# Layer 1's output product: the sums of two gate quarters made by accumulating DRAM transfers instead of VectorE

## The chip, the cores and the metric

The kernel runs on one core of a Trainium2 chip. The metric is the device time of one execution in microseconds (us), as a median over runs. The engines are TensorE (PE; its weight loads are PEld), VectorE (DVE), ScalarE (ACT), GpSimd (POOL) and SyncE (SP), which here issues nearly all transfers; a "q" behind an engine's name is its instruction queue.

## The reference

Causal attention with a decay, followed by two feed-forward layers. All is float32.

```python
def reference(**kwargs):
    attn_out = _attn_ref(**attn_kwargs)          # 4 batches, 8 heads, 576 positions, 64 wide
    B, H, S, D = attn_out.shape
    x = np.ascontiguousarray(attn_out.transpose(0, 2, 1, 3)).reshape(B * S, H * D)   # 2304 x 512
    x = _moe_ref(x=x, **moe_kwargs)              # h = x @ w_in; max(0.01 h, h) @ w_out, 512 -> 2048 -> 512
    return _moe2_ref(x=x, **moe2_kwargs)         # h = x @ w_in; (h * sigmoid(h)) @ w_out
```

## The kernel before

Tokens are processed in five stages that overlap: attention per head; the hidden product of layer 1 with its gate (line 960); the output product of layer 1 (line 1218); and the two products of layer 2 (lines 1525 and 1667). Each float32 operand of a product is split into a rounded part (a copy on ScalarE) and a residual (a subtraction on VectorE), and a product is three passes: rounded by rounded, and twice rounded by residual.

The hidden product runs over eight chunks of 256 or 320 tokens and 16 blocks of 128 features. It starts while attention is still running and fills TensorE's time between the heads. After each pair of blocks `gate` stores 128 x 2 x n gate values to the DRAM tensor `g1_d` (line 1055), 64 stores in all; `g1_d` has eight slabs (a slab is a pair of feature blocks), each over 2304 tokens.

The output product uses a scheme of seven products in place of eight. The tokens are cut into three groups of 768 (n = 0, 1, 2). A group's gate values are cut into quarters: "11" and "21" are the first and second 384 tokens with the first half of the features (slabs 0 to 3), "12" and "22" the same tokens with the second half (slabs 4 to 7). Each quarter comes as four pieces (s = 0 to 3) of 128 x 2 x 384 values, 384 KB, which `quarters` loads from `g1_d` (line 1091, tile gq). From them `made` and `prep` build the seven left operands, in place:

- operand 1 is "11", operand 2 is "12", operand 4 is "22";
- operand 5 is "21" + "22" (line 1117, the first operation of `made`);
- operand 6 is operand 5 minus "11" (line 1120);
- operand 7 is "22" minus operand 6 (line 1140), operand 3 is "12" minus operand 6 (line 1164).

All of these run on VectorE through the helper `sub`, so that the profile shows them under line 1357 (gq from gq): 16 per group, 48 in all. `prep` then splits each piece into the tile gs (line 1151 on ScalarE; the residual through the helper `less`, line 373, on VectorE). Four split buffers go round; a buffer comes free when TensorE has used it.

There are three sets of quarter buffers (`q_group`). "11" always uses set 0. "21" and "12" of a group use one and the same set, and "22" the other; the two change places from group to group. So "21" of group n+1 is loaded into the buffers that "22" of group n leaves, and "22" of group n+1 into those that "12" of group n leaves. "12" is used last in a group, by operand 3. The order of the loads is "11", "21", "22" of a group, with "12" of the group before it in front.

The order of all instructions on every engine is fixed when the program is built. A planner (`Plan`) plays the whole kernel through with a cost for every operation; coroutines (`hidden`, `quarters`, `preps`, `summed` and others) wait for signals, take buffers, and hand operations with a rank to an engine; the planner writes them out in the order in which the engines come free in its own time. A subtraction that may run on either VectorE or GpSimd goes to the one that would end it first. On the chip, each queue runs strictly in that order, and an instruction that waits holds up all behind it on its queue. The order of the seven operands of a group is in `G_TURN`: for the groups 1 and 2 it is 1, 6, 5, 2, 7, 4, 3.

GpSimd makes some key residuals for attention (line 369) until the end of attention, and nothing after that. It issues no transfer.

Of the kernel before, what the change touches and what calls it, by code (L numbers as in the profile page):

```python
# [13 lines left out]
ALU = mybir.AluOpType  # L14
# [43 lines left out]
)  # L58
SPLITS = 4
INPUT_AT = 5  # L60
X_ON = "d"
SET_B = ("h", "h", ("acc", 0), ("acc", 1))


# [8 lines left out]
TB = 384  # L73
# [14 lines left out]
class Plan:  # L88
# [90 lines left out]
    def wait(self, *names):  # L179
        def step(resume):  # L180
            missing = [n for n in names if n not in self.seen]
            if not missing:
                resume()
                return
            left = [len(missing)]

            def one():
                left[0] -= 1
                if not left[0]:
                    resume()  # L190

            for n in missing:
                self.waiting.setdefault(n, []).append(one)

        return step
# [8 lines left out]
    def signal(self, name):  # L204
        self.seen[name] = True
        for fn in self.waiting.pop(name, []):
            fn()
# [79 lines left out]
def fused_kernel(ctx, tc, qt, kt, va, vb, ft, w1, wi2, wo2, out):  # L287
    nc = tc.nc
# [8 lines left out]
    SF = FF // 4  # L297
# [769 lines left out]
    def quarter(grp, s):  # L1067
        return w2t["q", Q_AT[grp] + s // 2][:, s % 2]

    def q_group(n, name):  # L1070
        return {"11": 0, "21": 1 + n % 2, "12": 1 + n % 2, "22": 2 - n % 2}[name]

    def quarters():

        yield wait("decoded")
        todo = [(0, "11"), (0, "21"), (0, "22")]
        for n in range(NG):
            todo += [(n, "12")]
            if n + 1 < NG:
                todo += [(n + 1, "11"), (n + 1, "21"), (n + 1, "22")]  # L1080
        for n, name in todo:
            i, j = int(name[0]) - 1, int(name[1]) - 1
            o = (2 * n + i) * TB
            grp = q_group(n, name)
            for s in range(SF):
                sg = j * SF + s
                yield wait(*[("g1", k, sg) for k, (o1, n1) in enumerate(CHUNKS) if o1 < o + TB and o1 + n1 > o])
                yield take(("q", grp, s), 1)

                def load(n, name, s, sg, o, t):  # L1090
                    yield dma(393e3, lambda: nc.sync.dma_start(out=t, in_=g1_d[sg, :, :, o:o + TB]), 0)
                    signal(("q", n, name, s))

                p.start(load(n, name, s, sg, o, quarter(grp, s)))

    g_order = sorted((7 * n + pos, n, q) for n in range(NG) for q, pos in G_TURN[n])
    gx = {}
# [14 lines left out]

    def made(n, s):

        a11, a21, a22 = (quarter(q_group(n, k), s) for k in ("11", "21", "22"))
        yield wait(("q", n, "21", s), ("q", n, "22", s))
        yield sub(2 * TB, a21, a21, a22, X_ON, 0, ALU.add)
        signal(("x5", n, s))
        yield wait(("gx", n, 1, s))
        yield sub(2 * TB, a11, a21, a11, "d", 0)  # L1120
        signal(("x6", n, s))
        q_used(n, "21", s, 2)

    def prep(n, q, s, i):
        a = {k: quarter(q_group(n, k), s) for k in ("11", "12", "21", "22")}
        t = w2t["s", i % SPLITS]
        src, name = None, None
        if q == 1:
            yield wait(("q", n, "11", s))
            src = a["11"]  # L1130
        elif q == 5:
            yield wait(("x5", n, s))
            src = a["21"]
        elif q == 6:
            yield wait(("x6", n, s))
            src = a["11"]
        elif q == 7:
            yield wait(("x6", n, s))
            yield wait(("x3", n, s))
            yield sub(2 * TB, a["11"], a["22"], a["11"], "d", 0)  # L1140
            src = a["11"]
        elif q == 4:
            yield wait(("q", n, "22", s))
            src = a["22"]
        elif q == 2:
            yield wait(("q", n, "12", s))
            src = a["12"]
        else:
            yield wait(("x3", n, s))
            src = a["12"]  # L1150
        yield act(2 * TB, lambda: nc.scalar.copy(t[:, 0], src), 0, 0.09)  # L1151
        yield less(2 * TB, t[:, 1], src, f32(t[:, 0]), "d", 0, PE_LAT)
        gx[n, q, s] = t, i
        signal(("gx", n, q, s))
        if q == 5:
            q_used(n, "21", s, 2)
        elif q == 7:
            q_used(n, "22", s, 2)
            q_used(n, "11", s, 1)
        elif q == 4:  # L1160
            q_used(n, "22", s, 2)
        elif q == 2:
            yield wait(("x6", n, s))
            yield sub(2 * TB, a["12"], a["12"], a["11"], "d", 0)
            yield wait(("gx", n, 6, s))
            signal(("x3", n, s))
        elif q == 3:
            q_used(n, "12", s, 1)
# [802 lines left out]
        decp["wo"] = wo_es.enter_context(tc.tile_pool(name="wop", bufs=1))  # L1971

    with tc.manual_schedule():
        for gen in (opening(), first_weights(), loads(), attention(), hidden(), quarters(), preps(), summed(), all_fills(),
                    second_input(), second_weights(), hidden2(), second_values(), summed2()):
            p.start(gen)
        p.run()
# [51 lines left out]
```

## Time and profile before

| | |
|---|---|
| median of 3 runs | 960.33 us (959.15 to 962.2) |
| profiled execution, whole | 963.02 us |
| its span, first to last instruction | 961.3 us |
| TensorE busy | 940.9 us (98%) |
| VectorE busy | 753.1 us (78%) |
| ScalarE busy | 610.8 us (64%) |
| GpSimd busy | 56.5 us (6%) |
| moved by transfers | 196.8 MB |

Times are from the start of the span. Durations are from the one profiled execution. A matmul's end is modelled, so that a busy TensorE may still have matmuls that run slowly. The granted clock is given as a share of full speed. The DMA share is the mean busy share of the 16 transfer engines; it can come out slightly above 1.

The output product of layer 1 lies between 392 and 607 us. Until 419 us hidden-product work is mixed into it, and from 578 us on the first product of layer 2.

### The profile page before, as it was taken

To read this page: it belongs to the slowest core of one execution; us is meant where nothing else is said; L and a number is where in the kernel's file an instruction comes from. 1 tells how busy PE (TensorE), PEld (TensorE's weight loads), DVE (VectorE), ACT (ScalarE), POOL (GpSimd) and SP (SyncE) were. 2 spreads that over 40 slices of the span, in tenths; PEclk is the share of its full clock that TensorE was granted. 3 is DMA by queue.
4 is the path that set the end of the run, shared out by engine and by line. 5 is a ranking of instruction groups with operands and counts; after the bars stand their busy time and mean duration, and the time that the engine had idled before them with its cause. 6 is when DMAs were issued, how large, how long until landed. Compare 5 with 4: busy or idle time off the path is not lost.

```text
span 961.3 us, 18261 instructions
## 1 busy us (share of the span) xinstructions
PE 940.9 (98%) x6483; PEld 891.6 (93%) x6483; DVE 753.1 (78%) x1782; ACT 610.8 (64%) x1382; POOL 56.5 (6%) x71
## 2 busy tenths in 40 slices
PE   9999999999999999999989999999999999999998
PEld 7777998999888889999989899999999999999998
DVE  6998786689688962979999779858544498888885
ACT  7978787788588854666546359547556674444442
POOL 2001221122022100000000000000000000000000
PEclk9999999999999999999999999999999999999999
DMA  7943553466777656994956685797766683544542
GB/s 202 290 136 89 165 168 95 131 227 215 243 223 241 194 166 224 370 359 161 344 206 185 221 256 177 266 325 236 287 218 208 221 261 112 152 132 139 147 127 72
DMA packets 160023, 196.80 MB, mean 205 GB/s; under 512 B 9638, under 2 KB 145982, under 8 KB 159900
## 3 DMA queue, kind: packets, MB, share of 16 engines
q1 hardware_dynamic: 159500, 195.24, 63.5%
q8 instruction: 51, 0.84, 0.3%
q10 hardware_dynamic: 432, 0.39, 0.1%
q14 instruction: 40, 0.33, 0.1%
HBM read 125.94 MB, written 69.65 MB: 203 GB/s over the span
## 4 chain that ended last, share of the span: by engine, by line
PE 68%; DVE 13%; DMA 9%; ACT 5%; issue 3%; SPq 2%; POOL 0%; DVEq 0%; ACTq 0%; POOLq 0%
PE m L1667 18%; PE m L1525 18%; PE acc L1218 10%; PE hpw L960 10%; PE sps L743 4%; PE av L892 4%; PE tps L824 3%; DMA gq<-g_d 3%; DVE gq L1357 2%; DMA wst<-in_wi_dram 2%; ACT sc L766 1%; DVE sc L723 1%; DVE gs L373 1%; ACT sc L776 1%; PE hps L960 1%
## 5 line engine op out<-in xcount | busy, mean ns | idle before, releaser
L960 PE MATMUL hpw<-ring,w 128*128 128x320 f32 (+1 forms) x1344 | 218.0, 303 | 0.1
L960 PEld LDWEIGHTS hpw<-ring,w 128*128 128x128 f32 x1344 | 191.0, 190 | 2.4 <-issue 1.4
L1218 PE MATMUL acc<-gs,w 128*128 128x384 f32 x1008 | 186.2, 344 | 7.1 <-DVE gs L373 5.4
L1218 PEld LDWEIGHTS acc<-gs,w 128*128 128x128 f32 x1008 | 180.5, 191 | 10.2 <-DVE gs L373 6.5
L1525 PE MATMUL m<-xc,w 128*128 128x384 f32 x1008 | 180.3, 339 | 0.6 <-ACT m L1551 0.6
L1525 PEld LDWEIGHTS m<-xc,w 128*128 128x128 f32 x1008 | 177.6, 188 | 1.4 <-ACT m L1551 1.0
L1667 PE MATMUL m<-w,gc 128*128 128x256 f32 x1512 | 178.6, 280 | 0.0
L1667 PEld LDWEIGHTS m<-w,gc 128*128 128x128 f32 x1512 | 178.4, 188 | 0.0
L358 ACT CAST gc<-g 128x512 fp32r<-128x512 f32 (+1 forms) x180 | 80.0, 490 | 86.7 <-DVE g L1357 52.2
L1151 ACT CAST gs<-gq 128x768 fp32r<-128x768 f32 x84 | 69.8, 836 | 61.0 <-PE acc L1218 31.2
L766 ACT ACTIVATE sc<-sc,st 128x576 f32<-128x576 f32 (+4 forms) x160 | 92.9, 581 | 24.6 <-DVE st L723 23.6
L723 DVE CUSTOM_DVE_ANT_0 sc<-sps,zmask 128x288 f32<-128x288 f32 (+4 forms) x160 | 71.0, 448 | 31.1 <-PE sps L743 23.8
L373 DVE TENSOR_TENSOR gs<-gq,gs 128x768 fp32r<-128x768 f32 x84 | 79.4, 952 | 17.5 <-ACT gs L1151 16.9
L373 DVE TENSOR_TENSOR gc<-g,gc 128x512 fp32r<-128x512 f32 (+1 forms) x180 | 89.8, 525 | 3.3 <-ACT gc L358 1.9
L824 PE MATMUL tps<-ident,sc 66*107 66x66 f32 (+3 forms) x480 | 68.0, 269 | 3.8 <-ACT sc L776 1.8
L1357 DVE TENSOR_TENSOR g<-g 128x256 f32<-128x256 f32 x144 | 58.3, 418 | 16.7 <-DMA g<-g_d 16.2
L743 PE MATMUL sps<-m,s 66*128 66x288 f32 (+9 forms) x288 | 67.4, 315 | 3.2 <-DMA g_d<-gw 1.7
L369 POOL TENSOR_TENSOR m<-qk,m 64x288 fp32r<-64x288 f32 (+1 forms) x56 | 51.4, 930 | 275.2 <-ACT m L358 145.0
L373 DVE TENSOR_TENSOR w<-w 128x512 fp32r<-128x512 f32 x84 | 55.6, 686 | 14.6 <-ACT w L1915 14.4
L824 PEld LDWEIGHTS tps<-ident,sc 66*107 66x107 f32 (+3 forms) x480 | 55.2, 151 | 10.9 <-ACT sc L776 3.6
L1915 ACT CAST w<-w 128x512 fp32r<-128x512 f32 x84 | 50.7, 620 | 19.0 <-DMA w<-w_d 18.3
L1053 ACT ACTIVATE gw<-hpw 128x320 f32<-128x320 f32 (+1 forms) x112 | 44.7, 409 | 27.0 <-PE hpw L960 23.5
(124 smaller groups left out, 1113.3 us busy)
## 6 DMA issues: line engine op xcount, KB each, us to landing
w<-w_d SPq DMA_DIRECT2D x84, 256.0 KB
gq<-g_d SPq DMA_DIRECT2D x48, 384.0 KB
g_d<-z SPq DMA_DIRECT2D x24, 768.0 KB
g<-g_d SPq DMA_DIRECT2D x36, 512.0 KB
w_d<-f SPq DMA_DIRECT2D x16, 896.0 KB
g_d<-gw SPq DMA_DIRECT2D x32, 320.0 KB
wst<-in_w_dram SPq DMA_DIRECT2D x17, 512.0 KB
g_d<-gw SPq DMA_DIRECT2D x32, 256.0 KB
```

Source lines behind the costliest of these rows:

```text
L358: ("act", act_cost(n, base), lambda: nc.scalar.copy(dst, src), 0.0),
L373: ("dve", dve_cost(n), lambda: nc.vector.tensor_tensor(dst, a, b, op=ALU.subtract), 0.0),
L723: yield dve(w, lambda: nc.vector.tensor_tensor_reduce(out=sc[0:qn, k0:k0 + w], in0=ps[0:qn], in1=zmask[0:qn, z0:z0 + w], scale=-0.125, sca ...
L743: nc.tensor.matmul(ps[0:qn], ht[x][:, qs], ht[y][:, k0:k0 + w], start=r == 0, stop=r == len(ops) - 1)
L766: yield act(kn, lambda: nc.scalar.activation(sc[0:qn, 0:kn], sc[0:qn, 0:kn], ACTF.Exp, scale=-1.0, bias=st[0:qn, 2 * i + a:2 * i + a + 1], ...
L824: nc.tensor.transpose(ps[0:k1 - k0, o:o + qn], ht["p"][i][0:qn, k0:k1], ident[0:qn, 0:qn])
L960: nc.tensor.matmul(dst, w[:, wi, c * 128:(c + 1) * 128], x(xi, c), start=(first_ and c == 0 and r == 0), stop=(c == KC - 1 and r == 2), sk ...
L1151: yield act(2 * TB, lambda: nc.scalar.copy(t[:, 0], src), 0, 0.09)
L1218: nc.tensor.matmul(dst, w[:, e, wi, j * 128:(j + 1) * 128], x[:, xi, e], start=start and s == 0 and e == 0 and r == 0, stop=stop and s == ...
L1357: ("dve", dve_cost(n), lambda: nc.vector.tensor_tensor(dst, a, b, op=op_), 0.0),
L1525: nc.tensor.matmul(dst, w[:, wi, c * 128:(c + 1) * 128], x[:, xi, c], start=start and c == 0 and r == 0, stop=stop and c == 1 and r == 2, ...
L1667: nc.tensor.matmul(banks[b][:, e], t[:, gi, a * 128:(a + 1) * 128], w[:, wi], start=begin and a == 0 and r == 0, stop=jp == NP // 2 - 1 an ...
```

## The change

The sum "21" + "22" is no longer made on VectorE. A new coroutine `added` issues, for each group and piece, one transfer from GpSimd's queue that adds the piece of "22" in `g1_d` to the piece of "21" in `g1_d`, in DRAM: twelve transfers of 384 KB. Each waits for the gate stores of both pieces. The planner counts 1.1 us of GpSimd and 10 us to the landing. `added` is started ahead of `quarters`.

The load of "21" now waits for its sum in place of the gate stores and brings operand 5 directly. In `made` the first VectorE operation goes, and with it the wait for the load of "22"; operand 6 needs "21" and the split of operand 1. Operand 5 needs only the load of "21".

```diff
+    def g1_made(n, i, sg):
+        o = (2 * n + i) * TB
+        return [("g1", k, sg) for k, (o1, n1) in enumerate(CHUNKS) if o1 < o + TB and o1 + n1 > o]
+
+    def added():
+        for n in range(NG):
+            o = (2 * n + 1) * TB
+            for s in range(SF):
+                yield wait(*g1_made(n, 1, s), *g1_made(n, 1, SF + s))
+                yield op("pool", 1.1, lambda: nc.gpsimd.dma_start(
+                    out=g1_d[s, :, :, o:o + TB], in_=g1_d[SF + s, :, :, o:o + TB], accum_op=ALU.add), 0, 10.0)
+                signal(("sum21", n, s))
...
-                yield wait(*[("g1", k, sg) for k, (o1, n1) in enumerate(CHUNKS) if o1 < o + TB and o1 + n1 > o])
+                yield wait(*([("sum21", n, s)] if name == "21" else g1_made(n, i, sg)))
...
-        a11, a21, a22 = (quarter(q_group(n, k), s) for k in ("11", "21", "22"))
-        yield wait(("q", n, "21", s), ("q", n, "22", s))
-        yield sub(2 * TB, a21, a21, a22, X_ON, 0, ALU.add)
-        signal(("x5", n, s))
-        yield wait(("gx", n, 1, s))
+        a11, a21 = (quarter(q_group(n, k), s) for k in ("11", "21"))
+        yield wait(("q", n, "21", s), ("gx", n, 1, s))
         yield sub(2 * TB, a11, a21, a11, "d", 0)
         signal(("x6", n, s))
...
         elif q == 5:
-            yield wait(("x5", n, s))
+            yield wait(("q", n, "21", s))
             src = a["21"]
...
-        for gen in (opening(), first_weights(), loads(), attention(), hidden(), quarters(), preps(), summed(), all_fills(),
+        for gen in (opening(), first_weights(), loads(), attention(), hidden(), added(), quarters(), preps(), summed(), all_fills(),
```

## Rows read from the trace of the kernel before

**Rows 1.** The page's first part: busy us, share of the span, instructions.

```profile
PE 940.9 (98%) x6483; PEld 891.6 (93%) x6483; DVE 753.1 (78%) x1782; ACT 610.8 (64%) x1382; POOL 56.5 (6%) x71
```

**Rows 2.** TensorE's timeline: start, us, operation, count, idle before and releaser.

```profile
394.10 0.97 PE L1218 MATMUL acc<-gs,w 128*128 128x384 f32 x4 [0.86 <-DVE w L373]
...
405.38 13.80 PE L960 MATMUL hpw<-ring,w 128*128 128x320 f32 x93
...
445.76 34.33 PE L1218 MATMUL acc<-gs,w 128*128 128x384 f32 x192 [0.97 <-DVE gs L373]
481.06 4.41 PE L1218 MATMUL acc<-gs,w 128*128 128x384 f32 x23 [0.97 <-DVE gs L373]
486.33 0.44 PE L1218 MATMUL acc<-gs,w 128*128 128x384 f32 x1 [0.85 <-ACT gs L1151]
488.07 59.15 PE L1218 MATMUL acc<-gs,w 128*128 128x384 f32 x324 [1.30 <-DVE gs L373]
549.36 29.16 PE L1218 MATMUL acc<-gs,w 128*128 128x384 f32 x155 [2.14 <-DVE gs L373]
```

**Rows 3.** Busy us by stretch; the last three columns: granted clock, DMA share, GB/s.

```profile
150.00:200.00 50.00, 49.90 (x412) 44.06 (x411) 33.66 (x125) 37.16 (x114) 6.12 (x8) 1.00 0.45 138
340.00:350.00 10.00, 9.97 (x78) 8.51 (x77) 3.60 (x8) 1.80 (x6) 0.00 (x0) 1.00 0.92 285
406.00:422.00 16.00, 16.00 (x107) 16.00 (x107) 10.27 (x20) 8.25 (x18) 0.00 (x0) 1.00 1.00 345
430.00:450.00 20.00, 19.03 (x108) 18.70 (x107) 19.83 (x27) 13.46 (x24) 0.00 (x0) 1.00 0.52 186
470.00:488.00 18.00, 14.94 (x81) 13.73 (x79) 17.93 (x27) 8.06 (x12) 0.00 (x0) 1.00 0.69 262
488.00:494.00 6.00, 5.93 (x25) 5.93 (x26) 4.45 (x9) 1.82 (x5) 0.00 (x0) 0.72 0.66 148
547.00:555.00 8.00, 5.86 (x24) 5.65 (x24) 6.74 (x9) 3.23 (x4) 0.00 (x0) 0.79 0.32 97
```

**Rows 4.** VectorE's timeline around the sums: start, us, operation, count, idle before.

```profile
386.27 7.17 DVE L1357 TENSOR_TENSOR gq<-gq 128x768 f32<-128x768 f32 x8 [4.66 <-DMA gq<-g_d]
...
475.98 3.56 DVE L1357 TENSOR_TENSOR gq<-gq 128x768 f32<-128x768 f32 x4
...
480.06 0.95 DVE L373 TENSOR_TENSOR gs<-gq,gs 128x768 fp32r<-128x768 f32 x1
...
543.95 3.56 DVE L1357 TENSOR_TENSOR gq<-gq 128x768 f32<-128x768 f32 x4
```

**Rows 5.** The chain of work that ended last, in order of time: start, us, what.

```profile
343.27 6.40 DMA w_d<-wf
...
409.75 6.62 DMA wst<-in_wi_dram
...
470.95 4.65 DMA gq<-g_d
...
531.82 8.29 DMA gq<-g_d
```

**Rows 6.** Groups by line: count, busy us, mean ns, idle before and its releasers.

```profile
L1357 DVE TENSOR_TENSOR gq<-gq 128x768 f32<-128x768 f32 x48 | 44.1, 950 | 5.7 <-DMA gq<-g_d 5.6
L369 POOL TENSOR_TENSOR m<-qk,m 64x288 fp32r<-64x288 f32 (+1 forms) x56 | 51.4, 930 | 275.2 <-ACT m L358 145.0 <-DMA qk<-in_qt_dram 67.7 <-PE hpw L960 20.0
```

**Rows 7.** Timeline: gate stores (L1055), last "22" load (L1091), GpSimd's last residual.

```profile
195.96 2.89 SPq L1055 DMA_DIRECT2D g_d<-gw  x2
...
329.53 2.15 SPq L1055 DMA_DIRECT2D g_d<-gw  x2
...
343.88 0.62 SPq L1055 DMA_DIRECT2D g_d<-gw  x1
...
421.47 0.52 SPq L1055 DMA_DIRECT2D g_d<-gw  x1
...
539.23 0.52 SPq L1091 DMA_DIRECT2D gq<-g_d  x1
333.41 1.56 POOL L369 TENSOR_TENSOR m<-qk,m 64x288 fp32r<-64x288 f32 x2 [7.58 <-PE hpw L960]
```

More of the change, by code (lines that the diff above doesn't have):

```diff
@@ L60 @@
 INPUT_AT = 5
-X_ON = "d"
 SET_B = ("h", "h", ("acc", 0), ("acc", 1))
```

## The prediction

> **What bounds the kernel now.** I read the page's first part, then the busy time by stretches, then TensorE's timeline in the stage that the change touches, and last what VectorE and the transfers did at its gaps. TensorE is busy 940.9 of 961.3 us [rows 1], so no change outside TensorE can give more than the 20.4 us of its idle time, and what a slow clock costs after idle time. The question is therefore which of its gaps the twelve sums cause. In the first product of the layer-1 output stage (line 1218) the timeline shows six gaps [rows 2]: 0.86 us at 393, 0.97 at 445, then 0.97, 0.85 and 1.30 between 480 and 488, and 2.14 at 547. That is 7.1 us. Five of the six end with a VectorE instruction, the sixth with a ScalarE split. After the last two groups of gaps the granted clock is 0.72 over 488 to 494 and 0.79 over 547 to 555 [rows 3], that is, TensorE ran part of the time at 1.2 instead of 2.4 GHz after it had stood idle. Lost there: 6 x 0.28 = 1.7 us and 8 x 0.21 = 1.7 us. So the stage holds 7.1 + 3.4 = 10.5 us that a better supply could give back.
>
> The gaps of 480 and 547 have the sums right ahead of them. VectorE runs four 128x768 operations on gq in a row from 475.98, and the residual (gs) that ends the TensorE gap at 481.06 starts on VectorE at 480.06, behind them; from 543.95 four more run, right before the gap that ends at 549.36 [rows 2, 4]. Those four at 475.98 are the adds of the second group, and they run so late because they wait for the "22" quarter: in the chain of waits a gq load of 4.65 us ends just before 475.98, and one of 8.29 us just before the operations of 540.14 [rows 5]. The "22" quarter of a group goes into the buffers that "12" of the group before has left, the last to be freed.
>
> **What the change removes.** Of 48 operations on gq, 0.950 us each [rows 6], the twelve adds go: 12 x 0.95 = 11.4 us of VectorE. They are worth only what they hold up.
> - First group: the eight operations from 386.27 to 393.4 [rows 4] are four adds and four subtractions. TensorE still has the hidden product to do until 419, and only the 0.86 us gap at 393 follows. I take the gap: -0.9 us (0 to -0.9). The 0.97 us at 445 I leave in place: the operations ahead of it there are subtractions for operands 7 and 3, which stay.
> - Second group: operands 5 and 6 now need only "21", which lies in the buffers of the older "22" and is loaded before "22" of its own group. So the wait for the late load goes with the adds. The three gaps, 3.1 us, and the clock loss behind them, 1.7: -4.8 us. Between its ends (0 if the next operand is as late, -4.8) I take the whole, because the four adds take 3.56 us of VectorE [rows 4] in just the 18 us (470 to 488) in which VectorE is busy 17.93 [rows 3], more than the 3.1 us of gaps.
> - Third group, by the same reasoning: 2.1 + 1.7 = -3.8 us (0 to -3.8).
> Together -9.5 us. What is late next is the subtraction 21-11, one operation instead of two, behind a load that stands four places further ahead on SP's queue.
>
> **What it adds.** Twelve transfers issued from GpSimd, 384 KB each, that add one piece of DRAM to another. The trace of before has no such transfer, so I bound it. The least is one plain transfer: where the queues are full (406 to 422, share 1.00) they move 345 GB/s [rows 3], so 393,216 bytes take 1.14 us of all 16 engines. The most is three passes (read the addend, read the target, write the target), 3.42 us. I take two passes, 2.3 us, half-way, since a plain load also reads once and writes once.
> - First group: the stores that its sums wait for are the last four of the third chunk, which ends at 195.96 [rows 7], in 50 us with a share of 0.45 [rows 3]: four sums, 9 us, fit in. Cost 0 (with the cover gone, one late transfer; the nearest row is the 6.40 us of the next point).
> - Second group: the sums follow the stores from 329.53 to 343.88 [rows 7], and meet the 896 KB store of folded weights that the chain waits for from 343.27 for 6.40 us [rows 5], in a stretch where the DMA share is 0.92 and VectorE is busy 3.60 of 10 us [rows 3], that is, stands and waits. Three sums start before it lands: from 0 to 3 x 3.42 = 10.3 us. TensorE's order is fixed, so a late softmax shows as a gap. I take one sum, 2.3 us, because the first has some ten emptier microseconds ahead of the store and the last comes behind it.
> - Third group: the stores end at 421.47 [rows 7], in the full stretch. Four sums are 4 x 2.3 = 9.1 us of transfer beside the loads of the second layer's weights, one of which (6.62 us from 409.75) stands in the chain [rows 5]. Covered: VectorE is idle 16 - 10.3 = 5.7 us in 406 to 422, and the share falls to 0.52 from 430 on [rows 3]. The uncovered rest is 3.4 us; from 0 to 4 x 3.42 - 5.7 = 8.0 us; I take half the rest, 1.7, as the last of the four can only start behind 421 and reaches into the emptier stretch.
>
> A sentence of the Trainium skill speaks against the change here: by "DMA: Bandwidth & Descriptors", section "Issuing engines are not separate DMA queues", transfers issued from GpSimd run on the same 16 engines as those of the SP queue and interleave with them. No run here shows that yet, because before has no transfer from GpSimd; by it the costs above stand, and without it they would be nothing and the time 950.8. By "Collectives: The Full Stack", section "The bandwidth ceiling", an add made by the transfer engines needs two source reads and goes at half the rate of a copy; worked out from that and from the row's 1.14 us a sum would be an estimated 2.3 us, and no run shows it yet.
>
> Waits: on GpSimd a sum stands in order before later key residuals (56 of 0.93 us, the engine idle 275 us before them [rows 6]); the last of these starts at 333.41 [rows 7], so only the sums of the first group and one of the second have any behind them, and keys are prepared up to three heads ahead: cost 0, at worst one late transfer, 6.4 us. On SP the load of "21" waits for its sum, and all later loads stand behind it; the last sum of the second group follows a store of 343.88 and the load of "22" right behind "21" is at 470.95; for the third group these are 421.47 and 539.23 [rows 5, 7]. Over 110 us each are enough for any price above. Cost 0.
>
> **Sum.** -9.5 + 2.3 + 1.7 = -5.5 us. The profiled execution took 963.0 us (span 961.3 and 1.7 around it), 2.7 above the median of 960.3; against it the sum gives 957.5, and on the median 954.8: I say 955.
>
> **Rivals.**
> 1. *Slower: the sums starve the stores and loads.* Place: the attention's end at 343 and the full queues of 409 to 430 [rows 3]. If a sum takes p us of all engines and nothing but VectorE's 5.7 us covers it, the cost is 3p + 4p - 5.7. It beats the gain of 9.5 by more than the measuring limit of 2.9 us (0.3%, about what a measurement of this kernel tells from no change) from p = 2.6 us on. At p = 3.0 the cost is 15.3 and the time 960.3 + 5.8 = 966. For it: the full share in 406 to 422, and the one weight buffer of the attention, which makes everything wait for the store. Against: the share of 0.52 behind, and that transfers in two queues need not stand behind each other.
> 2. *No change: the gap gets another owner.* VectorE is busy 19.83 of 20 us in 430 to 450 [rows 3] without a single add, and each group still has twelve subtractions and 28 residuals; if half the gaps come back with other releasers, the gain is 4.7, the cost 4.0, and the time 960. For it: the residuals also wait for ScalarE's splits, as at 486.33 [rows 2]. Against: in 470 to 488 the adds are the difference.
> 3. *The sums cost nothing,* since they fall into spare share: 960.3 - 9.5 = 950.8. For it: 0.45 and 0.52 around. Against: 0.92 and 1.00 where two of the three groups lie.
>
> **Chances.** Forecast (950.9 to 957.4) 0.50; rival 3 0.08; rival 2 0.17; rival 1 0.25. Faster by over 0.3%: 0.50 + 0.08 = 0.58; within: 0.17; slower: 0.25. The range runs from 950, rival 3, to 966, rival 1 at p = 3.0; its own part, for the likeliest case alone, is 951 to 957.4.
>
> **What would show it.** Right: 36 operations on gq instead of 48; no gap of TensorE before operands 5 and 6 of the second and third group, and a clock of 1.00 behind both places; a first product that ends some 7 us earlier counted from its start; a DMA share above 0.92 around 340 and a later end of the 896 KB store there. Wrong: the sums visible for much more than 3.4 us each, gaps around 343 to 360 or 422 to 450 longer than now, key residuals on GpSimd that begin late, or a "21" load that waits for its sum on SP. A slower clock around 350 or 445 would add to rival 1.

## The result and the profile after

The kernel after takes 967.63 us (967.24 to 968.34, 4 runs) against 961.27 us (959.15 to 963.14) of the kernel before: a ratio of 1.007 [1.0048, 1.0091], 0.7% slower. A second series gave 968.72 against 960.73 us (e5_after, below). The prediction said 955, 5.5 us less than before; it is 6.4 us more. Its first rival, 966 us, came within 2 us, in part by luck: it was worked out at 3.0 us for a sum, and it left out a loss that is there. One execution of e3 (below), the profiled one, took 4245 us in place of some 952, and no trace of e3 is read here. In the code of the kernel after the lines stand elsewhere: L1227 for L1218, L372 for L373, L1160 for L1151, L1366 for L1357, L357 for L358, L823 for L824, L891 for L892, L1534 for L1525.

The page's first part and its row for GpSimd's queue (packets, MB, share of 16 engines' time); beside them the group of operations on gq. They answer [rows 1, 6]:

```profile
PE 941.0 (97%) x6483; PEld 890.5 (92%) x6483; DVE 745.4 (77%) x1771; ACT 612.2 (63%) x1382; POOL 65.2 (7%) x82
...
q0 software_dynamic: 3264, 4.72, 3.3%
```

```profile
L1366 DVE TENSOR_TENSOR gq<-gq 128x768 f32<-128x768 f32 x36 | 33.9, 953 | 0.9 <-DMA gq<-g_d 0.6
```

VectorE does what was planned: 36 operations for 48, and their idle time in front falls from 5.7 to 0.9 us. TensorE is as busy as before. So all that was lost is idle time of TensorE, or time at a slow clock. The queue's row gives the price of a sum: 3.3% of 16 x 965.6 engine-microseconds is 510; divided by 12 sums and 16 engines, 2.66 us of all engines. That is the price in this place: in f3 and g3 (below), where sums run elsewhere, the share is 3.0%, 2.4 us a sum.

TensorE's timeline from 340 to 620 us: start, us, operation, count, and in brackets the idle time before it. It answers [rows 2]:

```profile
358.42 0.90 PE L823 MATMUL tps<-ident,sc 128*128 128x128 f32 x3 [7.63 <-ACT pf L357]
...
446.25 0.44 PE L1227 MATMUL acc<-gs,w 128*128 128x384 f32 x1 [1.43 <-ACT gs L1160]
...
451.51 8.14 PE L1227 MATMUL acc<-gs,w 128*128 128x384 f32 x36 [1.29 <-DVE gs L372]
460.27 122.97 PE L1227 MATMUL acc<-gs,w 128*128 128x384 f32 x695 [0.62 <-DVE gs L372]
```

The last line is the change's success: 695 matmuls in 123 us without a gap, where before stood the four gaps of 480 to 549. The first line is its failure: 7.63 us idle at the end of the attention. Busy time by stretch (PE, PEld, DVE, ACT, POOL; then granted clock, DMA share, GB/s), beside [rows 3]:

```profile
340.00:350.00 10.00, 10.00 (x79) 8.78 (x78) 4.46 (x10) 2.49 (x7) 1.75 (x2) 1.00 0.93 224
350.00:360.00 10.00, 2.37 (x16) 2.12 (x15) 2.21 (x5) 1.96 (x5) 0.88 (x1) 0.66 0.69 184
...
430.00:450.00 20.00, 17.68 (x97) 16.76 (x96) 13.35 (x20) 12.82 (x20) 2.64 (x3) 1.00 1.10 322
450.00:470.00 20.00, 18.10 (x92) 17.55 (x92) 19.35 (x27) 12.84 (x21) 0.00 (x0) 0.91 0.54 180
...
488.00:494.00 6.00, 6.00 (x36) 6.00 (x35) 5.97 (x10) 3.00 (x4) 0.00 (x0) 1.00 0.98 335
547.00:555.00 8.00, 8.00 (x48) 8.00 (x47) 6.54 (x9) 4.45 (x7) 0.00 (x0) 1.00 0.56 186
```

The slow clocks behind 488 and 547 are gone (0.72 and 0.79 before), and new ones have come behind the new gaps: 0.66 in 350 to 360, 0.91 in 450 to 470. In 430 to 450 the engines are full (1.10, before 0.52), and VectorE has become the one that stands (13.35 of 20 us, before 19.83). The chain of waits, in order of time, beside [rows 5], and ScalarE's timeline at its first step:

```profile
344.14 12.77 DMA w_d<-wf
...
425.75 9.57 DMA wst<-in_wi_dram
...
435.33 13.02 DMA w<-w_d
```

```profile
357.07 0.66 ACT L1721 ACTIVATE wf<-wst 128x512 f32<-128x512 f32 x1 [12.24 <-DMA w_d<-wf]
...
357.93 0.76 ACT L357 COPY pf<-tps 107x320 f32<-107x320 f32 x2
```

In before the same gap was short; TensorE's timeline there:

```profile
351.19 0.55 PE L824 MATMUL tps<-ident,sc 128*128 128x128 f32 x3 [1.21 <-ACT pf L358]
```

The gap of 7.63 us is made thus: the store of folded weights takes 12.77 us in place of 6.40; the next fold on ScalarE waits for its only buffer (12.24 us); the copies of softmax tiles that TensorE needs (pf) stand behind that fold on ScalarE's queue.

**Where the time went.** I read the start of the same matmul groups off TensorE's timeline: A, the av product of eight matmuls at about 181 us; B, the av product of twenty near 247; C and D, the next two such near 342 and 350; F, the first matmul of layer 2 near 575. For the kernel after, and for a twin of the kernel before whose tiles nearly all stand 64 bytes higher (f4, below; it runs at the pace of the kernel before):

```profile
180.43 0.87 PE L891 MATMUL av<-pf,v 128*64 128x256 f32 x8
...
249.53 2.49 PE L891 MATMUL av<-pf,v 107*64 107x320 f32 x20
...
345.76 2.49 PE L891 MATMUL av<-pf,v 107*64 107x320 f32 x20
...
362.92 2.73 PE L891 MATMUL av<-pf,v 107*64 107x320 f32 x20
...
583.08 1.22 PE L1534 MATMUL m<-xc,w 128*128 128x384 f32 x6
```

```profile
181.05 0.87 PE L892 MATMUL av<-pf,v 128*64 128x256 f32 x8
...
246.99 2.49 PE L892 MATMUL av<-pf,v 107*64 107x320 f32 x20
...
341.58 2.49 PE L892 MATMUL av<-pf,v 107*64 107x320 f32 x20
...
350.45 2.49 PE L892 MATMUL av<-pf,v 107*64 107x320 f32 x20
...
574.10 1.22 PE L1525 MATMUL m<-xc,w 128*128 128x384 f32 x6
```

The differences are the lengths of four stages. The first group's sums run in A to B, the second group's around C to D, the third group's in D to F, where the gains are too. In us, with the kernels of the next section, each from its profiled execution:

| kernel | sums in DRAM | A to B | B to C | C to D | D to F |
|---|---|---|---|---|---|
| before | none | 65.93 | 96.97 | 9.16 | 224.26 |
| f4, before + 64 bytes | none | 65.94 | 94.59 | 8.87 | 223.65 |
| f1, before + 32 bytes | none | 65.92 | 94.76 | 9.01 | 223.31 |
| after | all | 69.10 | 96.23 | 17.16 | 220.16 |
| f2, after + 32 bytes | all | 68.52 | 94.85 | 15.33 | 218.80 |
| e1, plain copies | all, as copies | 68.47 | 95.39 | 11.82 | 215.51 |
| g1 | first group | 69.00 | 95.97 | 8.93 | 221.91 |
| g2 | third group | 65.91 | 94.63 | 8.76 | 225.94 |
| e4 | first and third | 68.20 | 94.81 | 8.70 | 224.46 |
| f3 | all, second held back | 68.15 | 95.90 | 9.04 | 223.62 |
| g3 | all, first and second held back | 65.92 | 97.24 | 8.62 | 219.59 |

B to C holds a stall near 300 us that some executions have and some have not, with the sums or without (94.59 and 96.97 in the kernel before and its twin), so differences there say nothing. Each line is one execution. Two executions of one kernel differ by 0.7 to 0.8 us in A to B and C to D and by 1.0 in D to F (after and e5), and by as much as 2.7 in D to F (e2 with 221.88, e8 with 219.20); those read for g2 and e4 are the fastest of their kernels, that of e1 is the slowest. So a difference of 2 or 3 us in D to F needs the medians or the gaps beside it. After minus twin: +3.2 in A to B, +8.3 in C to D, -3.5 in D to F. The predicted places of loss and gain were right for the second and third group; the sizes were not, and the first group's place was missed.

### The profile page after: what moved, and what is told of

It reads as the page before. It is cut to its first block, busy times and chain, and to the rows that moved or that the text cites. A ratio compares the mean times of both kernels' runs of the same rounds, so it can differ in the third digit from the quotient of the medians.

```text
span 965.6 us, 18278 instructions
## 1 busy us (share of the span) xinstructions
PE 941.0 (97%) x6483; PEld 890.5 (92%) x6483; DVE 745.4 (77%) x1771; ACT 612.2 (63%) x1382; POOL 65.2 (7%) x82
## 3 DMA queue, kind: packets, MB, share of 16 engines
q0 software_dynamic: 3264, 4.72, 3.3%
## 4 chain that ended last, share of the span: by engine, by line
PE 75%; DVE 8%; DMA 8%; ACT 5%; issue 2%; SPq 1%; POOL 0%; DVEq 0%; ACTq 0%
PE m L1534 18%; PE m L1676 18%; PE acc L1227 16%; PE hpw L959 9%; PE av L891 4%; PE sps L742 4%; PE tps L823 3%; DMA qk<-in_kt_dram 2%; ACT sc L765 2%; DMA wst<-in_wi_dram 2%; DVE sc L722 1%; DMA w<-w_d 1%; DMA w_d<-wf 1%; ACT sc L775 1%; PE hps L959 1%
## 5 line engine op out<-in xcount | busy, mean ns | idle before, releaser
L1227 PE MATMUL acc<-gs,w 128*128 128x384 f32 x1008 | 184.2, 341 | 4.8 <-DVE gs L372 2.5
L1227 PEld LDWEIGHTS acc<-gs,w 128*128 128x128 f32 x1008 | 179.0, 189 | 7.3 <-DVE gs L372 3.3
L1534 PE MATMUL m<-xc,w 128*128 128x384 f32 x1008 | 180.1, 339 | 0.0
L1676 PE MATMUL m<-w,gc 128*128 128x256 f32 x1512 | 178.6, 280 | 0.0
L1534 PEld LDWEIGHTS m<-xc,w 128*128 128x128 f32 x1008 | 177.7, 188 | 0.5 <-ACT z L1572 0.2
L357 ACT CAST gc<-g 128x512 fp32r<-128x512 f32 (+1 forms) x180 | 80.6, 491 | 83.5 <-DVE g L1366 44.1
L1160 ACT CAST gs<-gq 128x768 fp32r<-128x768 f32 x84 | 70.0, 837 | 45.8 <-PE acc L1227 22.8
L372 DVE TENSOR_TENSOR gs<-gq,gs 128x768 fp32r<-128x768 f32 x84 | 79.7, 954 | 18.8 <-ACT gs L1160 18.4
L372 DVE TENSOR_TENSOR gc<-g,gc 128x512 fp32r<-128x512 f32 (+1 forms) x180 | 90.1, 527 | 3.3 <-ACT gc L357 2.1
L823 PE MATMUL tps<-ident,sc 66*107 66x66 f32 (+3 forms) x480 | 69.8, 273 | 10.1 <-ACT pf L357 7.6
L823 PEld LDWEIGHTS tps<-ident,sc 66*107 66x107 f32 (+3 forms) x480 | 55.5, 154 | 18.6 <-ACT pf L357 8.9
L372 DVE TENSOR_TENSOR w<-w 128x512 fp32r<-128x512 f32 x84 | 56.1, 688 | 18.6 <-ACT w L1924 18.4
L1366 DVE TENSOR_TENSOR g<-g 128x256 f32<-128x256 f32 x144 | 58.5, 420 | 13.8 <-DMA g<-g_d 13.4
L368 POOL TENSOR_TENSOR m<-qk,m 64x288 fp32r<-64x288 f32 (+1 forms) x55 | 49.4, 910 | 268.7 <-ACT m L357 137.6
```

Of the source, the lines that this page charges most:

```text
L357: ("act", act_cost(n, base), lambda: nc.scalar.copy(dst, src), 0.0),
L372: ("dve", dve_cost(n), lambda: nc.vector.tensor_tensor(dst, a, b, op=ALU.subtract), 0.0),
L823: nc.tensor.transpose(ps[0:k1 - k0, o:o + qn], ht["p"][i][0:qn, k0:k1], ident[0:qn, 0:qn])
L1227: nc.tensor.matmul(dst, w[:, e, wi, j * 128:(j + 1) * 128], x[:, xi, e], start=start and s == 0 and e == 0 and r == 0, stop=stop and s == ...
L1366: ("dve", dve_cost(n), lambda: nc.vector.tensor_tensor(dst, a, b, op=op_), 0.0),
L1534: nc.tensor.matmul(dst, w[:, wi, c * 128:(c + 1) * 128], x[:, xi, c], start=start and c == 0 and r == 0, stop=stop and c == 1 and r == 2, ...
```

## The experiments

The theories have letters in the expectations. A: the accumulating transfers cost by their place and length. B: any transfer that GpSimd issues there would cost the same. C: the new order of instructions costs. W: the gain comes from the wait for the late "22". D: it comes from the time of the twelve VectorE operations saved. A1 and L came up on the way: A1, that the first group's sums cost time in the attention; L, that the addresses of tiles set TensorE's pace.

**Is it the adding, or the transfers?** e1 copies "22" over "21" in DRAM where after adds, so operand 5 is made from "22" alone; the order on all engines is that of after.

```diff
-  out=g1_d[s, :, :, o:o + TB], in_=g1_d[SF + s, :, :, o:o + TB], accum_op=ALU.add), 0, 10.0)
+  out=g1_d[s, :, :, o:o + TB], in_=g1_d[SF + s, :, :, o:o + TB]), 0, 10.0)
```

> The twelve transfers copy the piece in place of adding it (so operand 5 lacks a summand); every engine's instruction order is that of the changed kernel, word for word. Theory A (the adding itself makes a transfer long: 2.66 us of all 16 engines each by the queue's share, against 1.14 us for a plain load): share of the GpSimd queue falls from 3.3% to about 1.5%, the 896 KB store of 344 us takes 8 to 10 us in place of 12.8, TensorE's gap at 358 falls from 7.6 to 3 to 4 us, time 961 to 964. Theory B (any transfer issued from GpSimd at this place holds up the others, adding or not): gap 7.6, time 967 to 968. Theory C (the new order of instructions, not the transfers): the same as B.

Measured: 954.81 us (950.73 to 959.09), ratio to before 0.9959 [0.9938, 0.998]. GpSimd's queue, TensorE's gap at the attention's end, and the first loss in A to B, on VectorE and then on TensorE:

```profile
q0 software_dynamic: 1344, 4.72, 1.5%
```

```profile
353.17 0.55 PE L823 MATMUL tps<-ident,sc 128*128 128x128 f32 x3 [2.78 <-ACT pf L357]
```

```profile
201.38 0.45 DVE L358 CAST m<-qk 64x576 fp32r<-64x576 f32 x1 [2.40 <-DMA qk<-in_kt_dram]
```

```profile
203.48 0.54 PE L742 MATMUL sps<-m,s 128*128 128x288 f32 x2 [1.61 <-DVE st L722]
```

The same bytes go in 1344 packets instead of 3264, and a copy takes 1.5% x 16 x 957.4 / 12 / 16 = 1.20 us of all engines. The gap is 2.78 instead of 7.63 us, and D to F is 8.1 us shorter than in the twin. So B falls for these two places, and C for the kernel as a whole: with the same order and the same issues from GpSimd it is faster than before, and faster than the 961 to 964 us that I expected of A. In A to B theory B holds: e1 loses 2.5 us there, as much as with adds. A load of keys is 2.40 us late for VectorE, and TensorE stands 1.61 us behind it.

**The second group away from the attention's end.** e2 holds GpSimd's queue before the second group's sums, by an operation on two elements per partition that reads a split of the first group's operand 2, made at about 430 us. e8 is the same kernel again. e3 and e6, one kernel run twice, hold the third group's sums as well, to about 485 us, with a second entry in `SUM_GATE`, `2: (1, 6, 0)`.

```diff
+    sgate = const.tile([128, 2], F32, name="sgate")
...
+    SUM_GATE = {1: (0, 2, 0)}
...
+            if n in SUM_GATE:
+                yield wait(("gx", *SUM_GATE[n]))
+                x = gx[SUM_GATE[n]][0]
+                yield op("pool", 0.2, lambda: nc.gpsimd.tensor_scalar(
+                    sgate, f32(x[:, 0, 0, 0:2]), 0.0, 1.0, op0=ALU.max, op1=ALU.min), 0)
```

> As the changed kernel, but the second group's four sums wait on GpSimd until the first piece of operand 2 of the first group has been split (about 430 us), so that none runs at the end of attention. Theory A and B (the transfers hold up the store at 344): the store takes 6.4 us again, TensorE's gap there is 1.2 us, minus about 6.4 us plus 1 for the clock behind it; time 960 to 962, less what the four sums cost at 430. Theory C (order): the gap at 358 stays at 7 to 8 us, time 967.

> Only the second group's sums held to about 430 us; in its first run here all eight late sums went out between 431 and 439 us. Theory A, with the price of 2.7 us of all engines for a sum: eight of them are 21 us of transfer in one place, gaps of 4 to 5 us between 443 and 456 as seen once, so 2 to 4 us slower than e6. If lateness there is covered, the same as e6.

> As the one before, and the third group's four sums wait until the first piece of operand 6 of the second group has been split (about 485 us), so that they leave the full queues of 420 to 450. Theory A and B: TensorE's gaps between 440 and 462 (4.2 us now) go down to 1 to 2, no gaps at operands 5 and 6 of the groups 2 and 3, time 952 to 957. If the sums cost the same wherever they stand, 959 to 962. Theory C: 965 to 968.

> The changed kernel with the second group's sums held to about 430 us and the third's to about 485, again, with a profile that can be read. Theory A: no gap over 1.5 us at 350 nor at the operands 5 and 6 of groups 2 and 3; 7 us faster than before (952 where before is 959), 12 to 16 us faster than the changed kernel.

Measured: e2 951.86 us, ratio 0.9928 [0.9902, 0.9953]; e8 953.88, 0.9925 [0.9896, 0.9953]; e3 951.78, 0.9928 [0.9906, 0.9949]; e6 953.22, 0.9917 [0.9886, 0.9947]. The gap at the attention's end was about 1 us in those read (0.89, 0.87 and 1.22 in e2, e8 and e6). That looked like the whole answer: 15 us better than after. It was not: TensorE's busy time was 927.4 us in e8, 13.5 less than in before and after, though it does the same work, and the padded kernels below show why. So the 951.86 us of e2, 8 under what I expected, are not the gate's alone. Taken among each other, e6 and e8 show no difference that can be told by where the third group's sums go once the second group's are away.

**Wait or VectorE time?** e7 is e6 plus one maximum of "21" with itself per piece on VectorE, which has the shape of the old add and changes no value.

```diff
-        yield wait(("q", n, "21", s), ("gx", n, 1, s))
+        yield wait(("q", n, "21", s))
+        yield sub(2 * TB, a21, a21, a21, "d", 0, ALU.max)
+        signal(("x5", n, s))
+        yield wait(("gx", n, 1, s))
```

> As the one before, with one VectorE operation of the old add's shape put back for every piece (the maximum of the piece and itself, so that nothing changes in it), before operands 5 and 6 are made: VectorE's 11.4 us come back, the wait for quarter 22 does not. Theory D (VectorE's time is what the adds cost): the gaps at operands 5 and 6 come back, 8 us slower than e6, as before the change. Theory W (the wait for the late load is what they cost): within 3 us of e6.

Measured: 953.6 us, ratio 0.9932 [0.9908, 0.9956], 0.4 us above e6 on the same chip (1.4 by the ratios). First the gap at the second group's operands in e6, then in e7; then the stretch of e7 where before has the gap of 547:

```profile
486.98 0.44 PE L1235 MATMUL acc<-gs,w 128*128 128x384 f32 x1 [2.82 <-ACT gs L1168]
```

```profile
490.63 0.44 PE L1238 MATMUL acc<-gs,w 128*128 128x384 f32 x1 [2.41 <-ACT gs L1171]
```

```profile
540.00:552.00 12.00, 12.00 (x70) 11.79 (x69) 12.00 (x16) 5.92 (x9) 0.00 (x0) 1.00 0.75 227
```

Twelve operations of VectorE are back, and D's 8 us do not come. At the third group VectorE is busy 12.00 of 12 us with them and TensorE has no gap: there it is W, the late load. At the second group e6 keeps a gap of 2.82 us, against what I expected of it, and e7 one of 2.41, so that the operations do not show there either. A loss of 1 or 2 us is not ruled out: D to F takes 222.93 us in e7 and 221.31 in e6, and both stand close to the 223.31 of f1, which has their addresses and no sums.

**The second group's sum back on VectorE,** the others in DRAM (e4), and after once more (e5):

```diff
-        for n in range(NG):
+        for n in (0, 2):
...
+        if n not in (0, 2):
+            yield wait(("q", n, "21", s), ("q", n, "22", s))
+            yield sub(2 * TB, a21, a21, a22, "d", 0, ALU.add)
```

> The second group's sum is made on VectorE again, as before the change; first and third group in DRAM. Theory A and B: the gap at 358 goes back to 1.2 us, and the gaps of 3.1 us at operands 5 and 6 of the second group come back with 1.7 us of slow clock: time 961 to 964. Theory C: 965 to 968.

> The changed kernel itself once more, on the chip of the three runs that follow, so that they can be compared with it and with before. If the loss belongs to the transfers' place (theory A), it is 5 to 9 us slower than before here too, with a TensorE gap of 7 to 8 us at 358. If the loss was the chip's or the execution's, it is within 3 us of before.

Measured: e4 965.85 us, ratio 1.0077 [1.0048, 1.0107]; e5 968.72 us, 1.0077 [1.0038, 1.0115]. In e4 the stage C to D is sound again (8.70 us), and still the kernel is slower than before. It is above the 961 to 964 us that I expected of A and in the range that I gave to C, which e1 had excluded. A with the second group alone as the culprit does not explain that: the other two must cost too.

**The addresses.** The small tile for the gate's result stands ahead of nearly all others, so the gated kernels' tiles lie 32 bytes higher (the slot that its 8 bytes per partition take; a trace shows no addresses). f1 is before with such a tile that nothing uses, f2 is after with it, f4 and h1 are before with 64 and 96 bytes (16 and 24 wide in place of 2). f3 is e2 with the gate's result in a statistics tile that is no longer needed, so that no address moves.

```diff
-    stats = [const.tile([128, 12], F32, name=f"st{i}") for i in range(ST_BUFS)]
+    sgate = const.tile([128, 2], F32, name="sgate"); stats = [const.tile([128, 12], F32, name=f"st{i}") for i in range(ST_BUFS)]
```

> The kernel before with one unused 32-byte tile ahead of the statistics tiles: every instruction, wait and transfer is the same, but nearly every on-chip tile stands 32 bytes higher. The two gated kernels had such a tile for their gate's result, and TensorE's busy time in them is some 928.5 us against 941 in the kernels before and after (the costliest product 173.5 against 179 us). Theory L (the address alone sets that pace): busy TensorE 927 to 931 us, ratio to before 0.986 to 0.990, about 949 us. Rival (the gates did it, or something else of those kernels): ratio 0.998 to 1.002, about 960 us.

> The kernel after with the same unused tile. If the loss of the sums in the attention's end and in the product's start is independent of the pace (theory A with L): 6 to 8 us above the padded kernel before, ratio to before 0.993 to 0.997, about 955 us, with a gap of 6 to 8 us at the end of the attention. If the gates were what made the gated kernels fast: ratio 1.005 to 1.009, about 967 us.

> The second group's four sums held on GpSimd until the second input's sums, as in the gated kernel, but the gate writes into a statistics tile that is no longer used, so that all tiles stand where they stand in the kernels before and after. Theory A with L: the gap at the attention's end is 0.8 to 1.5 us in place of 7, busy TensorE some 941 us, and the time 5 to 7 us under the kernel after: 961 to 963 us, ratio to before 1.000 to 1.003. If the gate alone made the gated kernels fast: ratio 0.991 to 0.995, about 953 us.

> The kernel before with an unused tile of 64 bytes in place of 32: the tiles stand 64 bytes higher. If what matters is whether the addresses are odd multiples of 32 bytes, the pace is that of the kernel before (busy TensorE 941 us, ratio 0.998 to 1.002). If any shift that parts the tiles otherwise will do: busy 928 us, ratio 0.986 to 0.990.

> The kernel before with an unused tile of 96 bytes ahead of the statistics tiles. If odd multiples of 32 bytes give TensorE its better pace: busy TensorE 928 to 930 us, ratio 0.987 to 0.991, like the padding of 32 bytes. If the 32-byte case was a single lucky place: busy 939 to 941 us, ratio 0.998 to 1.002, like the padding of 64.

Measured: f1 949.33 us, ratio 0.9893 [0.986, 0.9925]; f2 955.91, 0.998 [0.9956, 1.0003]; f3 962.79, 1.0026 [1.0007, 1.0045]; f4 959.82, 0.9998 [0.9976, 1.0019]; h1 959.01, 0.9988 [0.9972, 1.0005]. The costliest group of TensorE in layer 2, first in before, then in f1 and h1 (count, busy us, mean ns):

```profile
L1667 PE MATMUL m<-w,gc 128*128 128x256 f32 x1512 | 178.6, 280 | 0.0
```

```profile
L1667 PE MATMUL m<-w,gc 128*128 128x256 f32 x1512 | 173.4, 277 | 0.0
```

```profile
L1667 PE MATMUL m<-w,gc 128*128 128x256 f32 x1512 | 182.2, 283 | 0.0
```

32 bytes, and no other change, give 10 us; 64 and 96 give nothing that can be told. The other kernels with 32 bytes, e2, e6, e7, e8, f2 and g4, on four chips, all have TensorE busy 927 to 932 us. My guess of odd multiples of 32 falls with h1. With padding on both sides the sums cost 6.6 us (955.91 - 949.33), about as much as without it (6.4 and 8.0), and holding back the second group is worth 5.9 us (968.72 - 962.79, across two chips; 4.9 by the ratios to before), not 15. f3 is still above before: something else costs 3.8 us by the medians, 2.5 by the ratio.

**Each group alone and in another place.** g1 makes only the first group's sums in DRAM, g2 only the third's, by the edit of e4 with `(0,)` and `(2,)`. g3 makes all, but holds the first group's sums until a ring tile of the last heads is written, at about 350 us, where the engines have room, and the second group's as e2 does; its tile is 64 bytes wide. g4 is g3 with 32 bytes.

```diff
+            if n == 0:
+                yield wait(*x_ready(NCH - 1, 1))
+                late = f32(ring[NCH - 1][0](0, 1))[:, CHUNKS[-1][1] - 2:CHUNKS[-1][1]]
+                yield op("pool", 0.2, lambda: nc.gpsimd.tensor_scalar(
+                    sgate[:, 0:2], late, 0.0, 1.0, op0=ALU.max, op1=ALU.min), 0)
```

> Only the first group's four sums are made in DRAM (issued between 187 and 222 us, in the attention); the second and third group's stay on VectorE, addresses as before. My prediction gave the first group a gain of 0.9 us. Theory A1 (these four cost some 2.7 us in the attention, and give about 1 back at the first product's start): 960 to 963 us, ratio 1.001 to 1.004, with TensorE some 2 to 3 us later at 250 us. Rival (the attention hides them, as predicted): 957 to 959 us, ratio 0.997 to 0.999.

> Only the third group's four sums are made in DRAM; the first and second group's stay on VectorE, addresses as before. By my steps c and d this is where 3.8 us are gained and 1.7 spent: gap at 547 us gone, its slow clock too, and 957 to 958 us, ratio 0.996 to 0.998. Rival (the third group's sums, at 424 to 439 us, delay loads of the running group by as much as they save): gaps of 3 to 5 us between 430 and 470 us in place of 1, and 960 to 963 us, ratio 1.000 to 1.004.

> All twelve sums in DRAM, but the first group's held on GpSimd until the attention's last heads (a two-element operation that reads the ring tile written at some 350 us) and the second group's until the second input's sums (some 430 us). The tile for the two results is 64 bytes wide, so that the pace of TensorE is that of the kernel before. At 350 to 375 us the transfer engines were 18 to 49 % busy. Theory A1: the 2.7 us in the attention are not lost, 2 to 3 us under the kernel with the second group held alone, 959 to 961 us, ratio 0.999 to 1.001. Rival (the first sums then come too late for their loads): TensorE waits at 375 to 400 us, 963 us or more, ratio above 1.003.

> The same with the tile 32 bytes wide, so that TensorE runs at the pace of the padded kernel before. If both effects add: 10 us under the former, 948 to 950 us, ratio 0.988 to 0.990, which is the padded kernel before within 2 us. If the late first sums collide with loads: 952 us or more.

Measured: g1 962.65 us, ratio 1.0035 [1.0017, 1.0052]; g2 962.3, 1.0031 [1.0014, 1.0048]; g3 956.16, 0.9977 [0.9949, 1.0004]; g4 949.0, 0.9888 [0.986, 0.9916].

g1 bears out A1. A TensorE line of g1, and the stretch 186 to 245 in g1 and then in g3, where these sums are not there:

```profile
194.54 0.30 PE L742 MATMUL sps<-m,s 66*128 66x128 f32 x1 [0.71 <-DMA m<-cum_d]
```

```profile
186.00:245.00 59.00, 56.02 (x408) 51.27 (x409) 51.11 (x165) 48.41 (x129) 15.41 (x17) 1.00 0.80 227
```

```profile
186.00:245.00 59.00, 58.04 (x430) 54.53 (x427) 52.57 (x166) 49.13 (x131) 13.98 (x14) 1.00 0.68 217
```

TensorE waits for a load of decay rows that attention needs, and for softmax work; in e1 it was a load of keys. A mean share of 0.68 leaves room for four sums, but here a load that meets a sum comes after it is needed. Of the 3.1 us that A to B is longer, 2.0 are idle time of TensorE (2.98 against 0.97 in the twin). One thing stands beside this: the planner gives a key residual at 190 us to VectorE in every kernel with the early sums (GpSimd has 55 of them for 56). It is not the cause as far as the trace shows: VectorE's next operation starts 9.55 us behind A in g1 and 9.47 in the twin. A to B is longer by 2.2 to 3.2 us in every kernel with the early sums, copies included, and unchanged in g2, g3 and g4.

g2 shows the third group's price. ScalarE's splits of the output weights, first the longest such wait of the twin in this stretch, then those of g2 (L1930 is L1915 of before), and TensorE's gaps in g2 (L1233 is L1218):

```profile
408.21 0.62 ACT L1915 CAST w<-w 128x512 fp32r<-128x512 f32 x1 [1.05 <-DMA w<-w_d]
```

```profile
419.87 0.62 ACT L1930 CAST w<-w 128x512 fp32r<-128x512 f32 x1 [4.17 <-DMA w<-w_d]
...
431.92 0.62 ACT L1930 CAST w<-w 128x512 fp32r<-128x512 f32 x1 [1.42 <-DMA w<-w_d]
```

```profile
434.52 0.44 PE L1233 MATMUL acc<-gs,w 128*128 128x384 f32 x1 [2.50 <-ACT gs L1166]
...
447.94 35.67 PE L1233 MATMUL acc<-gs,w 128*128 128x384 f32 x192 [2.13 <-DVE gs L372]
...
490.90 69.31 PE L1233 MATMUL acc<-gs,w 128*128 128x384 f32 x391 [1.30 <-DVE gs L372]
```

The gap near 545 is gone, 391 matmuls run through to 560 us, where this view ends, as predicted; the gaps up to 491 stay, since the second group's adds are on VectorE. But the sums, issued at 411 to 428, delay the loads of output weights; their splits wait on ScalarE's queue, the splits of gs behind them; the wait is handed on to VectorE, which has the next subtractions late. TensorE's gaps from 430 to 448 sum to 5.2 us, against 0.7 in the twin, with a clock of 0.95 in 405 to 470 against 1.00. D to F is 2.3 us longer than in the twin, where my steps had it 2.1 shorter; the medians say 3.5 us slower than before.

g3 puts four sums where the engines have room. GpSimd's issues of g3:

```profile
349.70 3.85 POOL L1094 DMA_DIRECT2D g_d<-g_d  x4 [0.24 <-issue]
...
429.15 7.50 POOL L1094 DMA_DIRECT2D g_d<-g_d  x8
```

The stretch 350 to 360 in the twin and in g3:

```profile
350.00:360.00 10.00, 9.96 (x82) 8.71 (x82) 7.03 (x21) 6.36 (x18) 0.00 (x0) 1.00 0.44 146
```

```profile
350.00:360.00 10.00, 9.75 (x81) 8.28 (x80) 8.09 (x24) 6.45 (x18) 3.55 (x4) 1.00 0.94 141
```

The share rises from 0.44 to 0.94 and nothing waits for it: TensorE's longest gap from 345 to 405 us is 0.67 us, in the twin 0.92. g3 is 6.6 us better than f3 (956.16 and 962.79, on two chips; 4.7 by the ratios), more than I expected. A is borne out: the same twelve sums cost 6 to 8 us in one place and nothing that can be told in another. That they give something there is not shown: against before g3 gains 2.6 us, with an interval that just reaches no change, and with 32 bytes on both sides it is 0.3 us (949.0 in g4, 949.33 in f1). g4 is the fastest kernel here, but its lead over before and after comes from the addresses.

## Why the prediction was wrong

- **What bounds the kernel, and that the gaps of 480 and 547 belong to the wait for "22":** right. Both are gone, with their slow clocks. With a transfer that is cheap (e1) D to F is 8.1 us shorter; my steps give 9.5 - 1.7 = 7.8, closer than they deserve, since a copy takes half of what I charged for a sum. But the reason that I gave for taking the whole, VectorE's full time in 470 to 488, is not needed: e7 gives VectorE its operations back, and the gap of the third group stays away and that of the second does not grow. What the runs point to is the late load.
- **The price of a sum, 2.3 us:** a little small where the sums stand in the kernel after, 2.66, and nearly right elsewhere, 2.4 in f3 and g3. On its own this moves the sum by at most 0.36 us for each sum that is uncovered. The Trainium skill's rule in "Collectives: The Full Stack", section "The bandwidth ceiling", gave an estimated 2.3 as well; here the measurement decides, with 2.4 to 2.66 for an add against 1.20 for a copy. Its rule in "DMA: Bandwidth & Descriptors", section "Issuing engines are not separate DMA queues", agrees with the trace: with GpSimd's transfers added the share in 430 to 450 is 1.10, and SP's store of 343 takes twice as long.
- **First group, cost 0 and gain 0.9: failed.** The gain may be there (D to F of g1 is 1.7 us shorter than in the twin, within what two executions differ by), but 3 us are lost in A to B. The cover was read from the mean share of a stretch, 0.45 over 150 to 200; the four sums are spread over 187 to 222, since the last two follow key residuals on GpSimd's queue, and in the attention the question is whether one small load comes late, not whether the bytes fit in.
- **Second group, cost 2.3: failed, the largest miss.** The place, the store of 343 and TensorE's gap behind it were named. I took one sum of the three that start before it lands. The store grew by 6.37 us, 2.4 sums at 2.66, the gap of 1.21 us became one of 7.63, and with the slower clock behind it the stage is 8.3 us longer. My bound of 10.3 held.
- **Third group, cost 1.7: failed.** g2 loses 2.3 us where my steps have -3.8 + 1.7 = -2.1, so its cost is 1.7 + 4.4 = 6.1 us if the whole 3.8 came in, which no run shows by itself; my bound was 8.0. I set VectorE's idle 5.7 us against it as cover. It covered nothing, since the delay does not end at VectorE: it comes in on ScalarE's queue through the output weights, and VectorE's own idle time becomes a wait for that.
- **Rival 1** had the mechanism, the two places and the deciding price of 2.6 us. At 2.66 its working gives 7 x 2.66 - 5.7 = 12.9 of cost and 963.7 us. The first group's 3 us, which it left out too, are most of the rest to 967.63. That its 966 lies so near is luck: a price that was too high stood in for the place that was missed.
- **Order on GpSimd and SP, cost 0:** not contradicted. e1 has the same orders and is faster than before; its 2.5 us in A to B follow a late load, but no run has that order without the transfers.

What stays open: how the 3 us of A to B part between the transfers and the order, why the product with a shift of 32 bytes takes 3% less, and what the stall near 300 us is that some executions have with and without the sums.

## What to carry to other kernels

Here work moved from an engine to the transfer engines was not paid in their mean share but in the next load or store with a deadline. So look for the transfers that the chain of waits already holds, count every added transfer that starts before they land, and take them all. An idle engine was no cover for a late transfer, because another queue brought the delay in. Before a kernel with an added tile is compared, run its parent with the same tile and nothing else: here the tile alone was worth 10 us, more than everything that was under test.

## What the runs showed of the hardware

- An add made by the transfer engines from DRAM to DRAM takes 272 packets per 384 KB (3264 for twelve) against 112 for a copy (1344), and 2.66 (after) or 2.4 (f3, g3) against 1.20 us of all 16 engines (e1).
- Transfers in one queue slow those in the other: with three adds from GpSimd's queue started before it lands, SP's store of 896 KB takes 12.77 us in place of 6.40 (before); with copies (e1) it takes 7.94, and with those adds held back (f3) 6.29.
- The pace of TensorE depends on where the tiles stand: at the same granted clock of 1.00 the product of line 1667 is busy 173.4 us with nearly all tiles 32 bytes higher, against 178.6, 179.7 and 182.2 at 0, 64 and 96 bytes, and TensorE in all 928.9 us against 940.9.
